# Linear attention and two MLPs on one core: chunk 1's attention moved by a step, two more tiles lent to the weight ring, x stores moved by an f tile

## The chip, the cores and the metric

One NeuronCore of a Trainium2 chip runs the program alone. The metric is the device time of an execution in microseconds (us); of several runs the median counts.

## What is computed

The reference computes, for 4 batches of 8 heads with 576 positions of 64 numbers, a linear attention and two MLPs behind it (cut):

```python
q = exp(q - q.max(-1));  q = q / (q.sum(-1) + 1e-9)       # softmax over the 64 numbers
k = exp(k - k.max(seq)); k = k / (k.sum(seq) + 1e-9)      # softmax over the positions
kv = einsum('bhsd,bhse->bhde', k, v)
x  = einsum('bhsd,bhde->bhse', q, kv)    # -> 2304 tokens x 512
h = x @ w_in                             # first MLP, 512 -> 2048
x = (s * relu(h)**2 + b) @ w_out         # 2048 -> 512
h = x @ w2_in                            # second MLP, 512 -> 2048
out = (h * tanh(softplus(h))) @ w2_out   # 2048 -> 512
```

The MLP weights come as float64 and must be used at about float32 precision.

## The kernel before

**Numbers.** The float64 weights are read as pairs of int32 and turned into float32 on the chip (`bits`, lines 132 to 144: one operation on ScalarE, four on VectorE). Each float32 operand is then split into a high part (a cast on ScalarE, line 178) and a low part (a difference on VectorE, line 175), and a product is three passes on TensorE, high by high, high by low and low by high (`passes`, line 185).

**First MLP.** The 2304 tokens are cut into five chunks (512, 256, 512, 512, 512), and the 2048 hidden numbers into 16 f tiles of 128. One f tile of one chunk is a step, 80 in all, and `n` counts them. At step n the kernel computes h of step n+2 (`emit_h`), its squared relu `r` and the split of that (`gh`, `gl`), and the y product of step n (`emit_y`), which is summed over the 16 steps of a chunk in four PSUM banks. At a chunk's end `y_out` copies the banks to `ys` and stores them to DRAM (`yd`). Sixteen weight tiles w0 to w15, of 128 x 2048 numbers (1 MB) each, hold the first MLP's weights; each holds two members, `wi` of one f tile and `wo` of another (`members`), and is read last by the last chunk at two late steps. During chunk 0 the weights arrive by SyncE's queue (`raw`), become float32 (`t`) and are split (`w`).

**Attention.** The attention of chunk c runs inside the steps of chunk c-1, for four head pairs (hp) one after the other. The stages att1 to att5 (maximum of k and q, differences and exponentials, sums, k by v on TensorE, a transpose of q to `qt`, and at last the product `x` with its copy to `xn`) are hung on steps by the table at line 855, as are the loads of k, v and q on SyncE's queue. For chunk 1 the first step of head pair hp is `2*hp+3`. `x_split` then makes `xh` and `xl` from `xn`, which the h matmuls of chunk 1 read.

**Second MLP.** Its weights are prepared on the side in the steps after 24: units of 1024 numbers a partition are read, converted, summed as a Strassen product of 2 x 2 blocks needs it, split into `umem` (in the tag w7) and stored to DRAM (`wdi` for the first, `wdo` for the second matrix) by GpSimd's queue, two stores a unit (line 332). The second MLP runs on pairs of chunks, (0, 2) and (3, 4), with seven products (P1 to P7) in place of eight: `h_unit` for each of eight tiles F, 42 matmuls of 512 columns each, and then `y_pair`. Its operands are `xoP` (x in seven combinations). Chunk 1 is done last, in the plain way.

**The ring.** The prepared weights come back in pieces `rw` of 1 MB or 768 KB, in order of use, by GpSimd's queue (lines 416 and 419). `ring_load` takes the tag that came free first, `ring_next` hands a piece out. The ring begins while chunk 4's steps run: pieces 0 and 1 go into the tags last and ws0, piece 2 into w7, which still holds `umem`; pieces 3 and 4 take last and ws0 again, and piece 5 gets ws1 when the raw y of the pair has been used there. From then on four tags go round. The tags w8 to w15 become the tiles g of F = 0 to 7, so w12 and w13 belong to F = 4 and 5.

**x of the second pair.** While the h tiles of pair 0 run, `b_steps(1, 0, put_dram)` builds the seven operands of the second pair for the lower half, splits each into `ghb` and `glb` and stores both to DRAM (line 386) on SyncE's queue. `g_tiles` gives these, and the `ghy`, `gly` of `y_pair` after them, three buffers each in turn, so that the fourth waits until the store out of the first has landed. For F from 2 to 7 this takes 1, 1, 1, 2, 2 and 1 of seven puts in the order P1, P7, P2, P6, P5, P4, P3; the upper half (`b_load(1, 1, "w7")`) is loaded behind F = 7.

The order of the instructions on each engine is made by a scheduler from these calls; instructions that go through `pin` or `keep_in_program_order` keep their order.

Of the kernel before, what the change touches and what calls it, by code (L numbers as in the profile page):

```python
# [31 lines left out]
def kernel(  # L32
# [22 lines left out]
    NF = DFF // P  # L55
# [8 lines left out]
    NU = NF // 2  # L64
# [24 lines left out]
    def segments(c):  # L89

        rq = CHUNKS[c] // P
        t, p0, found = T0[c], 0, []
        while p0 < P:
            b, s = divmod(t, S)
            n = min(P - p0, (S - s) // rq)
            found.append((b, p0, n, s))
            p0, t = p0 + n, t + n * rq
        return found


    def pin(ins):
        tc.keep_in_program_order(ins)
# [236 lines left out]
    def b_load(pair, kb, tag):  # L339

        t = (ws if tag.startswith("ws") else wp).tile([P, 4, CM], F32, tag=tag, name=f"b{pair}_{kb}")
        c0, c1 = PAIRS[pair]
        for spot, c, kk in ((0, c0, kb), (1, c0, 2 + kb), (2, c1, 2 + kb), (3, c1, kb)):
            nc.sync.dma_start(out=t[:, spot], in_=y_dram[c][:, kk, :])
        b_raw[kb] = t
# [49 lines left out]
    for pair in range(len(PAIRS)):  # L395
        ring += [("wi", F, i) for F in range(NU) for i in range(2)]
        ring += [("wo", r, i) for r in Y_ORDER for i in range(2)]
    RING = ("last", "ws0", "ws1")
    ring_t, ring_free, ring_done, ring_out = {}, ["last", "ws0", "w7"], [], set()

    def ring_load():
        ring_free.extend(ring_done)
        ring_done.clear()
        tag = ring_free.pop(0)
        if tag in ring_out:
            ring_out.discard(tag)
            return
        i = ring_at[0]
        ring_at[0] += 1
        if i >= len(ring):  # L410
            return
        t = (ws if tag.startswith("ws") else wp).tile([P, 2, 4, 2, P], F32R, tag=tag, name=f"rw{i}")
        z, a, b = ring[i]
        if z == "wi":
            o = slice(5, 8) if b else slice(0, 4)
            pin(nc.gpsimd.dma_start(out=t[:, :, 0:o.stop - o.start], in_=wi_dram[a][:, :, o]))
        else:
            t = t.rearrange("p i f h d -> p (i f h d)")
            pin(nc.gpsimd.dma_start(out=t, in_=wo_dram[b][:, BLOCK[a]].rearrange("p f i h d -> p (f i h d)")))
            t = t.rearrange("p (f i h d) -> p i f h d", f=4, i=2, h=2)  # L420
        ring_t[i] = (t, tag)

    def ring_more(tag):
        ring_free.append(tag)
        ring_load()

    def ring_next():
        t, tag = ring_t.pop(ring_at[1])
# [15 lines left out]
    def h_unit(pair, F):  # L444

        s1 = xp.tile([P, CM], F32, tag=f"xn{F % 2}", name=f"s1_{pair}_{F}")
        s2 = xp.tile([P, CM], F32, tag=f"xn{2 + F % 2}", name=f"s2_{pair}_{F}")
        s3 = rp.tile([P, CM], F32, tag="r", name=f"s3_{pair}_{F}")
        g = wp.tile([P, 4, CM], F32, tag=f"w{NU + F}", name=f"g{pair}_{F}")
        g_all[F] = g  # L450

        def mm(r, w, b):
            ps = h_bank(f"{r}_{pair}_{F}")
            for kb in range(2):
                passes(
                    ps, (w[:, kb, b, 0], w[:, kb, b, 1]), (x_op[r][:, 0, kb], x_op[r][:, 1, kb]),
                    kb == 0, kb == 1,
                )
            return ps

        def add(out, a, b):
            nc.vector.tensor_tensor(out=out, in0=a, in1=b, op=ALU.add)  # L462

        def mish(spot, src):
            nc.scalar.activation(out=g[:, spot], in_=src, func=AF.Mish)  # L465

        w = ring_next()
        p1 = mm("P1", w, 3)
        nc.scalar.copy(out=s1, in_=p1)
        p6 = mm("P6", w, 1)  # L470
        add(s2, s1, p6)
        p7 = mm("P7", w, 2)
        add(s3, s2, p7)
        p5 = mm("P5", w, 0)
        add(s2, s2, p5)
        ring_load()
        w = ring_next()
        p2 = mm("P2", w, 0)
        add(s1, s1, p2)
        mish(0, s1)  # L480
        p4 = mm("P4", w, 1)
        add(s1, s3, p5)
        mish(2, s1)
        add(s3, s3, p4)
        mish(1, s3)
        p3 = mm("P3", w, 2)
        add(s2, s2, p3)
        mish(3, s2)
        diff3(g)
        ring_load()  # L490

    TO3 = tuple(("P2", F) for F in (1, 3, 4, 5, 7)) + tuple(("P6", F) for F in (1, 3, 5))
# [62 lines left out]
    def turn(pair, k):  # L555

        j, r = divmod(k, 4)
        ps = ps_y.tile([P, DM], F32, tag=f"y{2 + k % 2}", name=f"o{pair}_{k}")
        for dr in range(2):
            for i in range(2):  # L560
                o = (2 * i + dr) * P
                nc.tensor.transpose(ps[:, o:o + P], c_all[pair][dr, j][i][:, r * P:(r + 1) * P], ident)
        if r % 2 == 0:
            o_t[pair] = cv.tile([P, 2 * DM], F32, tag=f"t{k // 2 % 2}", name=f"os{pair}_{k}")
        t = o_t[pair].rearrange("p (i d) -> p i d", i=2)
        (nc.vector.tensor_copy if r % 2 else nc.scalar.copy)(out=t[:, r % 2], in_=ps)
        if r % 2:
            rows(PAIRS[pair][j], r - 1, r + 1, t)
# [6 lines left out]
    rest_x, rest_w, rest_h, rest_g = {}, {}, {}, {}  # L575
    RN = CHUNKS[REST2]
    rest_seq = sorted([(2 * F, "wi", F) for F in range(NU)] + [(2 * F + LEAD2, "wo", F) for F in range(NU)])
    REST_TAGS = tuple(f"w{i}" for i in (0, 1, 2, 3, 4, 5, 7)) + RING

    def rest_x_load():  # L580
        t = cv.tile([P, 2 * DM], F32, tag="t0", name="rx")[:, 0:NK * RN].rearrange("p (k n) -> p k n", k=NK)
# [5 lines left out]
    def rest_load(i):  # L587
        _, z, F = rest_seq[i]
        tag = REST_TAGS[i % len(REST_TAGS)]
        t = (ws if tag.startswith("ws") else wp).tile([P, 2, 4, 2, P], F32R, tag=tag, name=f"rw_{z}{F}")  # L590
# [253 lines left out]
    def at(slot, what, fn, *args):  # L844
        todo.setdefault((slot, what), []).append((fn, args))
# [6 lines left out]
    for c in range(1, NC):  # L852
        wide = CHUNKS[c - 1] == CM
        for hp in range(NP):
            s = (c - 1) * NF + 3 * hp - 1 if c > 1 else 2 * hp + 3
            b = segments(c)[-1][0]
            if b > segments(c - 1)[-1][0]:
                first = c == 1 and hp == 0
                at(-2 if first else s - ((4 if hp else 5) if c > 1 else 2), "load", kv_load, b, hp)
                at(-2 if first else s + (0 if wide and c > 1 else 1), "load", v_load, b, hp)  # L860
            else:
                b = None
            at(-2 if c == 1 and hp < 2 else s - (2 if hp else 4), "load", q_load, c, hp)
            o = (0, 1, 2, 3, 4) if wide else (0, 1, 3, 4, 5)
            at(s + o[0], "att1", att1, b, c, hp)
            at(s + o[1], "att2", att2, b, c, hp)
            at(s + o[2], "att3", att3, b, c, hp)
            at(s + o[3], "att4_mm", att4_mm, b, c, hp)
            at(s + o[3], "att4", att4, b, c, hp)
            at(s + o[4], "att5_mm", att5_mm, b, c, hp)  # L870
# [5 lines left out]
    L0 = (NC - 1) * NF  # L876
# [11 lines left out]
    for kb in range(2):  # L888
        at(L0 + 2 * kb, "load", b_load, 0, kb, f"ws{kb}")
        for i in range(7):  # L890
            at(L0 + 2 + 5 * kb + i, "unit", b_next, kb)
    for s in (2, 9, 11):
        at(L0 + s, "load", ring_load)
    at(L0 + 14, "load", ring_more, "ws1")

    h_slot = {}
    for m in range(LEAD, NS):
# [31 lines left out]
    for n in range(NS):  # L929
        c, f = steps[n]  # L930
# [30 lines left out]

    for pair in range(len(PAIRS)):
        for F in range(NU):
            if (pair, F) == (1, 0):
                ring_more("w7")
            if F == NU - 2:
                ring_out.add("w7")
            if (pair, F) != (0, 0):
                h_unit(pair, F)
            if pair:  # L970
                turn(pair - 1, F)
            elif F == 1:
                b_load(1, 0, "w15")
                steps_b = b_steps(1, 0, put_dram)
            elif F > 1:
                for i in range((F > 4) + (F < NU - 1)):
                    next(steps_b, None)
                if F == NU - 1:
                    assert not ring_out
                    b_load(1, 1, "w7")  # L980
        if pair == 0:
            steps_b = b_steps(1, 1, put_both)
            more = [(next, steps_b)] * 7
        else:
            rest_x_load()
            more = [(rest_load, i) for i in range(7)]
        more.reverse()

        def one_more():
            fn, arg = more.pop()  # L990
            fn(arg)

        y_pair(pair, one_more)
    for i in range(7, len(REST_TAGS)):
        rest_load(i)
    for f in range(LEAD2):
        rest_h_mm(f)
    turned, loaded = 0, len(REST_TAGS)
    for f in range(NF):
# [10 lines left out]
        while loaded < len(rest_seq):  # L1010
            _, z, F = rest_seq[loaded - len(REST_TAGS)]
            if 2 * F + 1 - (LEAD2 if z == "wi" else 0) > f:
# [37 lines left out]
```

## Time and profile before

| | us |
|---|---|
| median of 3 runs | 848.21 (848.2, 848.21, 848.71) |
| the profiled execution | 845.78 |
| its span, from the first instruction to the last | 844.0 |
| TensorE (PE) busy | 821.0 (97%) |
| VectorE (DVE) busy | 605.8 (72%) |
| ScalarE (ACT) busy | 436.2 (52%) |
| GpSimd (POOL) busy | 108.7 (13%) |

All times of the trace count from the span's start in the profiled execution. PE is the matmul pipe and PEld its weight loads, SP is SyncE, and "SPq" or "POOLq" the issue of a DMA on that engine's queue. A number in square brackets behind an instruction is the time that its engine stood idle before it, and behind the arrow what ended that. Matmuls overlap a little: one of 512 columns starts 0.227 us after the one ahead of it, though each is shown as 0.39 us long. The mean granted clock of TensorE is 0.998 of full speed.

### The profile page before, as it was taken

The page shows a single profiled execution, that of the slowest core. Times are in us where ns is not written, and L with a number is a line of the kernel's source. Part 1 is how long each engine was busy: PE and PEld are TensorE (multiplying, and loading weights), DVE is VectorE, ACT ScalarE, POOL GpSimd, SP SyncE. Part 2 cuts the span into 40 slices and gives each one's busy share as a digit, 9 for nine tenths or more (in the row PEclk, how much of TensorE's full clock was granted, in tenths as well). Part 3 has the DMA queues.
Part 4 walks back from the last instruction along what each step waited for, and adds up shares of the span by engine and source line. Part 5 has one row for each costly group of instructions (what it writes and reads, how often), then busy time and mean ns, then how long its engine had stood idle before and what let it go on. Part 6 is the DMA issues. An engine that isn't in the chain of part 4 may idle for free.

```text
span 844.0 us, 11482 instructions
## 1 busy us (share of the span) xinstructions
PE 821.0 (97%) x4056; PEld 660.0 (78%) x4056; DVE 605.8 (72%) x1145; ACT 436.2 (52%) x771; POOL 108.7 (13%) x193
## 2 busy tenths in 40 slices
PE   4999999999999999999999989999999999999998
PEld 2444787998888888888888878878888888888897
DVE  7879987668677777867778656789775655976411
ACT  3636668567566566565566433455452333444322
POOL 4000000000011111111221211101111110112110
PEclk9999999999999999999999999999999999999999
DMA  8995122245465466558767498977778776688891
GB/s 219 301 365 176 33 66 92 61 151 165 158 210 196 180 216 223 185 165 273 234 210 228 144 342 236 280 257 249 233 244 262 237 199 202 218 299 283 255 373 62
DMA packets 90473, 179.01 MB, mean 212 GB/s; under 512 B 26928, under 2 KB 45104, under 8 KB 86832
## 3 DMA queue, kind: packets, MB, share of 16 engines
q0 software_dynamic: 30256, 112.73, 41.3%
q1 hardware_dynamic: 59072, 64.50, 24.5%
q10 hardware_dynamic: 1088, 1.05, 0.4%
q8 instruction: 32, 0.52, 0.2%
q14 instruction: 25, 0.20, 0.1%
HBM read 131.60 MB, written 46.66 MB: 211 GB/s over the span
## 4 chain that ended last, share of the span: by engine, by line
PE 61%; issue 27%; POOL 4%; DVE 3%; DMA 3%; ACT 1%; POOLq 0%; SPq 0%; DVEq 0%; ACTq 0%
PE P L185 24%; PE h L185 7%; PE y L185 6%; PE h L223 4%; PE y L266 3%; PE rh L185 3%; PE ry L185 3%; POOL wdo L332 2%; POOL wdi L332 2%; PE P3y L185 1%; PE P6y L185 1%; PE P5y L185 1%; PE P4y L185 1%; PE P2y L185 1%; PE P7y L185 1%
## 5 line engine op out<-in xcount | busy, mean ns | idle before, releaser
L185 PE MATMUL y<-gh,w 128*128 128x512 f32 (+1 forms) x584 | 179.6, 372 | 0.0
L185 PE MATMUL h<-xh,w 128*128 128x512 f32 (+1 forms) x568 | 173.5, 372 | 1.3 <-ACT xh L178 1.0
L185 PE MATMUL P<-xoP,rw 128*128 128x512 f32 x672 | 155.7, 390 | 2.7 <-DMA rw<-wdi 2.7
L185 PEld LDWEIGHTS P<-xoP,rw 128*128 128x128 f32 x672 | 125.8, 188 | 29.0 <-DVE s L462 3.1
L185 PEld LDWEIGHTS y<-gh,w 128*128 128x128 f32 x584 | 106.8, 189 | 18.7 <-issue 1.0
L185 PEld LDWEIGHTS h<-xh,w 128*128 128x128 f32 x568 | 104.5, 191 | 19.3 <-ACT xh L178 1.4
L462 DVE TENSOR_TENSOR s<-s,P 128x512 f32<-128x512 f32 x112 | 75.2, 686 | 51.8 <-PE P L185 35.8
L178 ACT CAST ghy_P<-g 128x512 fp32r<-128x512 f32 x112 | 69.7, 623 | 76.8 <-DVE gly_P L175 28.8
L185 PE MATMUL y<-gl,w 128*128 128x512 f32 (+1 forms) x292 | 106.9, 368 | 0.0
L185 PE MATMUL h<-xl,w 128*128 128x512 f32 (+1 forms) x284 | 105.3, 372 | 0.4 <-DVE xl L175 0.4
L175 DVE TENSOR_TENSOR gly_P<-g,ghy_P 128x512 fp32r<-128x512 f32 x112 | 76.1, 689 | 31.3 <-ACT ghy_P L178 29.2
L185 PE MATMUL P<-ghy_P,rw 128*128 128x512 f32 x224 | 87.2, 391 | 0.0
L465 ACT ACTIVATE g<-s 128x512 f32<-128x512 f32 x64 | 39.9, 632 | 89.9 <-DVE s L462 89.7
L248 ACT ACTIVATE r<-h 128x512 f32<-128x512 f32 (+1 forms) x80 | 43.9, 551 | 37.5 <-PE h L185 33.1
L185 PEld LDWEIGHTS y<-gl,w 128*128 128x128 f32 x292 | 55.1, 189 | 9.7 <-issue 0.5
L175 DVE TENSOR_TENSOR gl<-r,gh 128x512 fp32r<-128x512 f32 (+1 forms) x73 | 45.8, 629 | 21.8 <-ACT gh L178 21.5
L185 PEld LDWEIGHTS h<-xl,w 128*128 128x128 f32 x284 | 54.3, 191 | 9.2 <-DVE xl L175 0.6
L175 DVE TENSOR_TENSOR umem<-u,umem 128x512 fp32r<-128x512 f32 x64 | 41.7, 687 | 17.2 <-ACT umem L178 17.2
L178 ACT CAST umem<-u 128x512 fp32r<-128x512 f32 x64 | 36.6, 617 | 32.2 <-DVE u L319 32.0
L185 PEld LDWEIGHTS P<-ghy_P,rw 128*128 128x128 f32 x224 | 42.1, 188 | 8.4
L251 ACT ACTIVATE r<-r 128x512 f32<-128x512 f32 (+1 forms) x80 | 46.9, 589 | 1.9
L185 PE MATMUL P<-gly_P,rw 128*128 128x512 f32 x112 | 44.7, 399 | 0.3 <-DVE gly_P L175 0.3
(168 smaller groups left out, 1264.9 us busy)
## 6 DMA issues: line engine op xcount, KB each, us to landing
rw<-wdo POOLq DMA_DIRECT2D x28, 1024.0 KB, 5.2
wdi<-umem POOLq DMA_DIRECT2D x32, 512.0 KB, 3.7
wdo<-umem POOLq DMA_DIRECT2D x32, 512.0 KB, 3.7
rw<-wdi POOLq DMA_DIRECT2D x16, 1024.0 KB, 6.3
rw<-wdi POOLq DMA_DIRECT2D x16, 768.0 KB, 5.8
raw<-in_moe_w_in_dram SPq DMA_DIRECT2D x16, 512.0 KB, 9.4
raw<-in_moe_w_out_dram SPq DMA_DIRECT2D x16, 512.0 KB, 9.5
ur<-in_moe_w_in_dram SPq DMA_DIRECT2D x16, 512.0 KB, 4.2
```

The costliest lines, as they stand in the source:

```text
L175: pin(eng.tensor_tensor(out=lo, in0=src, in1=hi.bitcast(F32), op=ALU.subtract))
L178: pin(nc.scalar.copy(out=hi, in_=src))
L185: mm = nc.tensor.matmul(out=ps, lhsT=x, rhs=y, start=start, stop=stop)
L223: nc.tensor.matmul(out=h_ps[m], lhsT=wl[:, o], rhs=x_whole[kk], start=kk == 0, stop=kk == NK - 1,)
L248: op = nc.scalar.activation(out=r, in_=h_ps.pop(m), func=AF.Relu)
L251: nc.scalar.activation(out=r, in_=r, func=AF.Square)
L266: nc.tensor.matmul(out=ps, lhsT=wl[:, o], rhs=gl, start=f == 0, stop=False)
L332: nc.gpsimd.dma_start(out=to.rearrange("p b h d -> p b (h d)"), in_=u_mem[0][:, half].rearrange("p b h d -> p b (h d)"),)
L462: nc.vector.tensor_tensor(out=out, in0=a, in1=b, op=ALU.add)
L465: nc.scalar.activation(out=g[:, spot], in_=src, func=AF.Mish)
```

## The change

Three things, each by a number or a list of the plan.

- Chunk 1's attention begins at step `2*hp+2` of chunk 0 in place of `2*hp+3`, with all its loads.
- The ring begins with five pieces in five tags: last, ws0, w12 (at step 76), w13 and ws1 (at step 77). The tags w12 and w13 are used once and dropped (`ring_out`). The tag w7 joins behind F = 0 of pair 0 (before: with the third piece) and leaves at F = 6.
- The puts for F = 2 to 7 are 1, 1, 2, 2, 2 and 0, where the last call before did nothing.

```diff
--- before.py
+++ after.py
@@ -395,8 +395,7 @@
     for pair in range(len(PAIRS)):
         ring += [("wi", F, i) for F in range(NU) for i in range(2)]
         ring += [("wo", r, i) for r in Y_ORDER for i in range(2)]
-    RING = ("last", "ws0", "ws1")
-    ring_t, ring_free, ring_done, ring_out = {}, ["last", "ws0", "w7"], [], set()
+    ring_t, ring_free, ring_done, ring_out = {}, [], [], set()
 
     def ring_load():
         ring_free.extend(ring_done)
@@ -404,7 +403,10 @@
         tag = ring_free.pop(0)
         if tag in ring_out:
             ring_out.discard(tag)
-            return
+        else:
+            ring_into(tag)
+
+    def ring_into(tag):
         i = ring_at[0]
         ring_at[0] += 1
         if i >= len(ring):
@@ -419,10 +421,6 @@
             pin(nc.gpsimd.dma_start(out=t, in_=wo_dram[b][:, BLOCK[a]].rearrange("p f i h d -> p (f i h d)")))
             t = t.rearrange("p (f i h d) -> p i f h d", f=4, i=2, h=2)
         ring_t[i] = (t, tag)
-
-    def ring_more(tag):
-        ring_free.append(tag)
-        ring_load()
 
     def ring_next():
         t, tag = ring_t.pop(ring_at[1])
@@ -575,7 +573,7 @@
     rest_x, rest_w, rest_h, rest_g = {}, {}, {}, {}
     RN = CHUNKS[REST2]
     rest_seq = sorted([(2 * F, "wi", F) for F in range(NU)] + [(2 * F + LEAD2, "wo", F) for F in range(NU)])
-    REST_TAGS = tuple(f"w{i}" for i in (0, 1, 2, 3, 4, 5, 7)) + RING
+    REST_TAGS = tuple(f"w{i}" for i in (0, 1, 2, 3, 4, 5, 7)) + ("last", "ws0", "ws1")
 
     def rest_x_load():
         t = cv.tile([P, 2 * DM], F32, tag="t0", name="rx")[:, 0:NK * RN].rearrange("p (k n) -> p k n", k=NK)
@@ -852,7 +850,7 @@
     for c in range(1, NC):
         wide = CHUNKS[c - 1] == CM
         for hp in range(NP):
-            s = (c - 1) * NF + 3 * hp - 1 if c > 1 else 2 * hp + 3
+            s = (c - 1) * NF + 3 * hp - 1 if c > 1 else 2 * hp + 2
             b = segments(c)[-1][0]
             if b > segments(c - 1)[-1][0]:
                 first = c == 1 and hp == 0
@@ -889,9 +887,9 @@
         at(L0 + 2 * kb, "load", b_load, 0, kb, f"ws{kb}")
         for i in range(7):
             at(L0 + 2 + 5 * kb + i, "unit", b_next, kb)
-    for s in (2, 9, 11):
-        at(L0 + s, "load", ring_load)
-    at(L0 + 14, "load", ring_more, "ws1")
+    for s, tag in ((2, "last"), (9, "ws0"), (12, "w12"), (13, "w13"), (13, "ws1")):
+        at(L0 + s, "load", ring_into, tag)
+    ring_out.update(("w12", "w13"))
 
     h_slot = {}
     for m in range(LEAD, NS):
@@ -961,9 +959,9 @@
 
     for pair in range(len(PAIRS)):
         for F in range(NU):
-            if (pair, F) == (1, 0):
-                ring_more("w7")
-            if F == NU - 2:
+            if F == (pair == 0):
+                ring_into("w7")
+            elif F == NU - 2:
                 ring_out.add("w7")
             if (pair, F) != (0, 0):
                 h_unit(pair, F)
@@ -973,7 +971,7 @@
                 b_load(1, 0, "w15")
                 steps_b = b_steps(1, 0, put_dram)
             elif F > 1:
-                for i in range((F > 4) + (F < NU - 1)):
+                for i in range((0, 0, 1, 1, 2, 2, 2, 0)[F]):
                     next(steps_b, None)
                 if F == NU - 1:
                     assert not ring_out
```

What the scheduler makes of it stands here for three places; in these rows a number behind a name is that of the chunk, head pair or F, and a last one counts buffers.

GpSimd's queue near the end of the first MLP, before, with `umem`'s last stores (`wdo_103`) and pieces 0 to 5 of the ring:

```order
L332 DMA wdo_103<-umem 128x4x256 x2
L416 DMA rw_4026<-wdi_94 128x2x1024
L332 DMA wdo_103<-umem 128x4x256 x8
L416 DMA rw_4367<-wdi_94 128x2x768
L332 DMA wdo_103<-umem 128x4x256 x6
L416 DMA rw_4463<-wdi_95 128x2x1024
L416 DMA rw_4597<-wdi_95 128x2x768
L416 DMA rw_4629<-wdi_96 128x2x1024
```

And now:

```order
L332 DMA wdo_103<-umem 128x4x256 x2
L418 DMA rw_4026<-wdi_94 128x2x1024
L332 DMA wdo_103<-umem 128x4x256 x8
L418 DMA rw_4367<-wdi_94 128x2x768
L332 DMA wdo_103<-umem 128x4x256 x4
L418 DMA rw_4507<-wdi_95 128x2x1024
L332 DMA wdo_103<-umem 128x4x256 x2
L418 DMA rw_4549<-wdi_95 128x2x768
L418 DMA rw_4551<-wdi_96 128x2x1024
```

Piece 2 has moved ahead of the last two stores, and piece 3 (768) stands right behind them as before.

ScalarE where chunk 0 ends and chunk 1 begins, before (`ys` are the y copies of chunk 0, `xn_3` and `xh_3` the last head pair of chunk 1's x, `r` the relu of its first two h):

```order
L178 CAST w_1287<-t_458 128x2x512
L281 ACTIVATE ys_0_1235<-y_0_447,sb_s 128x512
L281 ACTIVATE ys_0_1238<-y_0_448,sb_s 128x512
L178 CAST w_1329<-t_479 128x2x512
L281 ACTIVATE ys_0_1241<-y_0_449,sb_s 128x512
L835 COPY xn_3_1118<-x_3_1115 128x256
L178 CAST xh_3_1144<-xn_3_1118 128x256
L178 CAST w_1387<-t_500 128x2x512
L281 ACTIVATE ys_0_1244<-y_0_450,sb_s 128x512
L248 ACTIVATE r_1176<-h_1163 128x256
L248 ACTIVATE r_1202<-h_1189 128x256
```

And now:

```order
L178 CAST w_1186<-t_433 128x2x512
L833 COPY xn_3_1080<-x_3_1077 128x256
L178 CAST w_1287<-t_458 128x2x512
L178 CAST xh_3_1144<-xn_3_1080 128x256
L281 ACTIVATE ys_0_1235<-y_0_447,sb_s 128x512
L281 ACTIVATE ys_0_1238<-y_0_448,sb_s 128x512
L281 ACTIVATE ys_0_1241<-y_0_449,sb_s 128x512
L178 CAST w_1329<-t_479 128x2x512
L751 ACTIVATE q_0_1042<-q_0_1042 128x512
L281 ACTIVATE ys_0_1244<-y_0_450,sb_s 128x512
L248 ACTIVATE r_1176<-h_1163 128x256
L248 ACTIVATE r_1202<-h_1189 128x256
```

The copy of `xn_3` has moved ahead of the ys and of one weight cast, an exponential of the next attention (`q_0`) ahead of the last ys, and the first `r` still stands behind all of them.

VectorE where `y_pair` of pair 0 begins, before (`glb` are the last two puts, `gly` the splits of g for P1, `s_0_7` the sums of F = 7, `g` differences of the g tiles):

```order
L175 TENSOR_TENSOR glbP_0_5123<-b_0_4727,ghbP_0_5122 128x512
L175 TENSOR_TENSOR gly_P_0_5212<-g_0_4564,ghy_P_0_5211 128x512
L462 TENSOR_TENSOR s_0_7_5129<-s_0_7_5128,P_0_7_5140 128x512
L351 TENSOR_TENSOR g_0_4564<-g_0_4564 128x512
L462 TENSOR_TENSOR s_0_7_5130<-s_0_7_5129,P_0_7_5148 128x512
L462 TENSOR_TENSOR s_0_7_5129<-s_0_7_5129,P_0_7_5156 128x512
L175 TENSOR_TENSOR gly_P_1_5222<-g_1_4660,ghy_P_1_5221 128x512
L462 TENSOR_TENSOR s_0_7_5128<-s_0_7_5128,P_0_7_5164 128x512
L175 TENSOR_TENSOR gly_P_2_5233<-g_2_4735,ghy_P_2_5232 128x512
L351 TENSOR_TENSOR g_1_4660<-g_1_4660 128x512
L351 TENSOR_TENSOR g_2_4735<-g_2_4735 128x512
L462 TENSOR_TENSOR s_0_7_5128<-s_0_7_5130,P_0_7_5156 128x512
```

And now:

```order
L175 TENSOR_TENSOR gly_P_0_5212<-g_0_4568,ghy_P_0_5211 128x512
L175 TENSOR_TENSOR gly_P_1_5222<-g_1_4664,ghy_P_1_5221 128x512
L351 TENSOR_TENSOR g_0_4568<-g_0_4568 128x512
L460 TENSOR_TENSOR s_0_7_5129<-s_0_7_5128,P_0_7_5140 128x512
L351 TENSOR_TENSOR g_1_4664<-g_1_4664 128x512
L460 TENSOR_TENSOR s_0_7_5130<-s_0_7_5129,P_0_7_5148 128x512
L175 TENSOR_TENSOR gly_P_2_5233<-g_2_4735,ghy_P_2_5232 128x512
L460 TENSOR_TENSOR s_0_7_5129<-s_0_7_5129,P_0_7_5156 128x512
L460 TENSOR_TENSOR s_0_7_5128<-s_0_7_5128,P_0_7_5166 128x512
L351 TENSOR_TENSOR g_2_4735<-g_2_4735 128x512
L460 TENSOR_TENSOR s_0_7_5129<-s_0_7_5129,P_0_7_5186 128x512
L460 TENSOR_TENSOR s_0_7_5128<-s_0_7_5130,P_0_7_5156 128x512
```

The second `gly` has moved ahead of the sums of F = 7 and the third one ahead of two of them; the sum that frees the bank of P5 (the last row of both) stands behind one more sum, and no longer behind a wait for P4's stores.

## Rows read from the trace of the kernel before

**Rows 1.** The page's part 1: busy us, share of the span, instructions.

```profile
PE 821.0 (97%) x4056; PEld 660.0 (78%) x4056; DVE 605.8 (72%) x1145; ACT 436.2 (52%) x771; POOL 108.7 (13%) x193
```

**Rows 2.** TensorE's waits: who waited for whom, us in total, times, longest.

```profile
PE P L185 <- DMA rw<-wdi: 2.7, 1, 2.7
...
PE h L185 <- ACT xh L178: 1.0, 1, 1.0
PE P1y L185 <- DVE s L462: 0.9, 1, 0.9
PE h L185 <- DVE xl L175: 0.4, 1, 0.4
```

**Rows 3.** Timeline of TensorE, 139 to 144 us.

```profile
139.15 0.71 PE L833 MATMUL x<-qt,bd 128*128 128x64 f32 x4
...
143.66 0.39 PE L185 MATMUL h<-xh,w 128*128 128x256 f32 x1 [0.31 <-ACT r L248]
```

**Rows 4.** Table by stretches: busy time of each engine, granted clock, DMA share, GB/s.

```profile
40.00:60.00 20.00, 20.00 (x48) 8.95 (x47) 16.10 (x23) 8.33 (x11) 0.00 (x0) 1.00 1.06 367
...
144.00:147.00 3.00, 3.00 (x17) 3.00 (x15) 1.72 (x4) 3.00 (x7) 0.00 (x0) 0.50 0.56 182
...
490.00:492.00 2.00, 2.00 (x9) 1.66 (x10) 0.72 (x2) 0.63 (x1) 0.00 (x0) 1.00 1.11 403
```

**Rows 5.** Timeline of TensorE, 467 to 492 us: start, us, instruction, idle before it.

```profile
467.79 0.39 PE L185 MATMUL y<-gh,w 128*128 128x512 f32 x1
...
478.45 4.24 PE L185 MATMUL P<-xoP,rw 128*128 128x512 f32 x18
...
489.94 2.31 PE L185 MATMUL P<-xoP,rw 128*128 128x512 f32 x9 [2.72 <-DMA rw<-wdi]
```

**Rows 6.** Timeline of GpSimd, 460 to 492 us.

```profile
467.09 1.50 POOL L332 DMA_DIRECT2D wdo<-umem  x2 [6.62 <-DVE umem L175]
475.23 1.50 POOL L332 DMA_DIRECT2D wdo<-umem  x2 [6.64 <-DVE umem L175]
482.40 1.42 POOL L416 DMA_DIRECT2D rw<-wdi  x2 [5.67 <-DMA wdo<-umem]
```

**Rows 7.** The page's part 6, DMA issues: count, KB each, us to landing.

```profile
rw<-wdi POOLq DMA_DIRECT2D x16, 1024.0 KB, 6.3
...
xdP<-glbP SPq DMA_DIRECT2D x7, 256.0 KB, 4.6
```

**Rows 8.** Timeline of SyncE's queue, 549 to 553 us.

```profile
550.18 1.11 SPq L386 DMA_DIRECT2D xdP<-glbP  x2
```

**Rows 9.** Timeline of VectorE, 556 to 561 us.

```profile
556.07 0.69 DVE L175 TENSOR_TENSOR gly_P<-g,ghy_P 128x512 fp32r<-128x512 f32 x1 [1.86 <-DMA xdP<-glbP]
...
559.08 1.88 DVE L462 TENSOR_TENSOR s<-s,P 128x512 f32<-128x512 f32 x3
```

**Rows 10.** Timeline of TensorE, 559 to 561 us.

```profile
559.82 0.50 PE L185 MATMUL P1y<-ghy_P,rw 128*128 128x512 f32 x1 [0.94 <-DVE s L462]
```

**Rows 11.** Timeline of ScalarE, 140 to 144 us.

```profile
140.55 0.37 ACT L835 COPY xn<-x 128x256 f32<-128x256 f32 x1
140.95 0.40 ACT L178 CAST xh<-xn 128x256 fp32r<-128x256 f32 x1
141.47 1.05 ACT L178 CAST w<-t 128x1024 fp32r<-128x1024 f32 x1
142.65 0.69 ACT L281 ACTIVATE ys<-y,sb_s 128x512 f32<-128x512 f32 x1
143.24 0.65 ACT L248 ACTIVATE r<-h 128x256 f32<-128x256 f32 x2
```

**Rows 12.** Timelines of VectorE (two rows) and TensorE (one), 49 to 132 us.

```profile
49.22 0.43 DVE L728 TENSOR_TENSOR kmx<-kb 128x256 f32<-128x256 f32 x1 [0.69 <-DMA kb<-in_k_dram]
...
127.26 2.35 DVE L175 TENSOR_TENSOR w<-t,w 128x1024 fp32r<-128x1024 f32 x2
...
131.62 0.50 PE L185 MATMUL y<-gh,w 128*128 128x512 f32 x1
```

## Prediction

> **What bounds the kernel now.** The page's first two parts come first: TensorE is busy for 97% of the span [rows 1], so there is little to win but its idle time, and no other engine's share says where that is. The table of TensorE's waits says it [rows 2]. Outside start-up three places matter: 2.7 us for a piece of the second MLP's weights (`rw`); 1.0 and 0.4 us for xh and xl where chunk 1's h matmuls begin, with 0.31 us for `r` behind them in TensorE's timeline [rows 3], 1.7 together; and 0.9 us where `y_pair` of the first pair begins. The table by stretches [rows 4] adds one cost that no wait shows: from 144 to 147 us, right behind the second of these places, the granted clock is 0.50, the lower of the two levels (1.2 GHz), so 3.0 us of work there is worth 1.5 us at 2.4 GHz. So all that can be had at the three places that the change touches is about 2.7 + 1.7 + 1.5 + 0.9 = 6.8 us.
>
> **Part by part.**
>
> *Two ring pieces into w12 and w13.* The wait of 2.72 us stands at 489.94 [rows 5]. GpSimd issues pieces 2 and 3 at 482.40 [rows 6], 5.67 us after it was ready for them, when the last store out of `umem` had landed, since piece 2 goes into that tile's tag (w7) and its queue is in order. After the change piece 2 goes into w12 and stands ahead of the last two stores, so it can be issued behind the pair at 467.09, at 468.6, if w12 is free: w13's last reader is a y matmul that ends at 468.2 [rows 5], and w12's is one step older. Landing takes 6.3 us [rows 7], so 474.9, with 12 us to spare before 487.2, where TensorE comes to it. Piece 3 follows the stores at 475.23 (476.7, in by 483). It is needed after piece 2's matmuls, so after 487.2. The whole wait of 2.7 us goes. What is late next: piece 4, in ws1, free when TensorE has done with it in the stretch from 478.45 [rows 5]; one more landing puts it at about 485, and it belongs to F=2, ten microseconds on. The tiles w12 and w13 become g of F=4 and 5, long after. Nothing is added to any engine; the count of DMAs stays. Below nothing I see no way for this term; its ends are -2.0 (some of it comes back as a shorter wait for piece 3) and -2.9, and I take **-2.7**.
>
> *x stores one f tile sooner.* Before, the four stores of the puts P4 and P3 are issued together at F=6, the low halves from 550.18 to 551.3 [rows 8], and two of the three g buffers that `y_pair` wants are theirs. VectorE stands 1.86 us for `xdP<-glbP` until 556.07, then works without a gap, and the subtraction that frees the PSUM bank of P1y is the first of three that begin at 559.08 [rows 9]; TensorE begins at 559.82 after 0.94 us [rows 10]. After, P4's stores leave at F=5 and P3's alone at F=6: `gly` of F=1 needs no store, and only that of F=2 waits, for P3's low half, issued at about 550.1 and landing after 4.6 us [rows 7], at 554.7. From there VectorE's new order has gly_2, three of the sums, one g difference and then the freeing sum: six instructions at about 0.6 us, so it ends near 558.4. TensorE is ready at 559.82 - 0.94 = 558.88. The wait goes with 0.5 us to spare. One store pair instead of two shares the queue then, which speaks for the 4.6; at the 5.9 us that the store at 550.18 took until 556.07 the sum ends at 559.7 and nothing is won. Two puts at F=5 cost VectorE and ScalarE nothing in sum. `b_load` of kb 1 goes later by about one tile of h work, since w7 is now held through F=7; its result is used by `y_pair`'s later puts, so I price it at nothing; if it were late the first `xo` put would be. Ends -0.0 and -0.9; I take **-0.9**, since the median of seven such stores stands for it and one late store against.
>
> *Chunk 1's attention one step sooner.* Nothing is added; every stage, with the DMAs of kb, v and q, moves ahead one step of chunk 0. At the border TensorE's `x` matmul of head pair 3, at 139.15 [rows 3], stands ten y matmuls sooner in the new order, each 0.227 us (18 of that size in 4.24 us with the last one's 0.39 [rows 5]), at about 136.8. Then xn and xh no longer stand behind three ys, and the waits for xh and xl (1.4 us) go. But ScalarE is in order, and the new order still has ahead of the first `r` of chunk 1, from xn at 136.9 on: xn, a weight cast, xh, three ys, another cast, an exp and the last ys. From start to next start the rows give 0.40 for xn, 0.52 for xh, 1.18 for a cast and 0.59 for a ys [rows 11]; the exp, 512 columns like a ys, I put at 0.55. That is 0.40 + 1.18 + 0.52 + 1.77 + 1.18 + 0.55 + 0.59 = 6.2 us: `r` begins near 143.1, where before it began at 143.24 and TensorE went on at 143.66 [rows 3]. So the wait does not vanish but turns into one for `r`, of 1.4 us in one piece (143.66 - 1.71 = 141.95 is where TensorE would be without any). Gain 0.2 to 0.4 us. The clock is the second half: whether it falls again to 1.2 GHz behind one wait of 1.4 us nothing in the trace decides. It fell behind 1.7 us in three pieces within 2.4 us, and it did not behind the longer wait of 2.72 us: in 490 to 492 it is 1.00 [rows 4]. I let it fall again. Ends: +1.0 (the same waits and a little more), and -3.2 (all 1.7 and the clock's 1.5). I take **-0.3**, the sum from ScalarE's rows.
>
> The Trainium skill, "TensorE: Matmul & The Clock Gate", Part 1, says that the clock follows recent activity in a window that runs freely and is not tied to the program; by it the fall behind the border could come or not from one program order to the next. The pair of places above agrees with it, a longer wait without a fall and a shorter one with it; by it the sum would be the rival below about as well as mine.
>
> Sum: -2.7 - 0.9 - 0.3 = -3.9 us. The profiled execution took 845.78 us (span 844.0 and 1.8 around it), 2.4 us less than the median 848.21; taking the difference off both, the changed kernel's profile should be near 841.9 and its median near **844.3**.
>
> **The rivals.**
>
> *The clock stays up at the border.* The lower clock's 1.5 us is then saved as well, but VectorE's new order puts the lo part of chunk 1's first g further back, behind two more attention operations and a weight difference of 1.2 us, so part of it returns as a wait for `gl`. Between 843.6 (1.0 us from this part in place of 0.3) and 842.8 (1.8, the whole of it). For it: one shorter wait. Against: any wait may do. Without any wait there (3.2) it would be 841.4.
>
> *The stores buy nothing.* The low half takes 5.9 us as one of them did, and the 0.9 stays, 845.2. For it: [rows 9]. Against: half the stores.
>
> *The ring turns into a wait for piece 3 or 4.* 845.6, with a gain of 1.4 in place of 2.7. Against it stand 4 us or more of spare time at both.
>
> *Slower: VectorE stands for k.* VectorE already waited 0.69 us for a k tile at 49.22 [rows 12], and in the new order this maximum stands ahead of the conversion of weight tile 4. The stretch 40 to 60 has the DMA engines at a share of 1.06 [rows 4], full. A step of chunk 0 is under 139.15/16 = 8.7 us. If the k tile lands no sooner, VectorE stands up to 0.69 + 8.7 = 9.4 us, and as the conversions follow one another it comes out at TensorE once it is over their slack: tile differences end at 129.61 and matmuls at 131.62 use them [rows 12], so from 2.0 us on. At the full price TensorE loses 7.4 us and, with a clock fall of 1.5, the sum is -3.6 + 8.9 = +5.3, 853.5; at half of the 7.4 it is 849.8. Against it: SyncE issues these k loads ahead of one raw pair now, so they will land sooner too.
>
> The Trainium skill, "DMA: Bandwidth & Descriptors", section "Issuing engines are not separate DMA queues", says that loads from every engine's queue run on the same 16 DMA engines and interleave; by it an earlier issue into a full stretch would not be an earlier landing in full, which speaks for the slower case. The share of 1.06 in that stretch agrees that they are full; no row shows how much a place on the queue is worth.
>
> **How the numbers follow.** My forecast, 844.3, gets 0.46; the clock that stays up 0.28 (with 841.4 inside it at 0.04); stores that buy nothing 0.12; a new ring wait 0.06; slower 0.05, of which 0.02 lands inside 0.2%; that the change leaves all as it was 0.03. A measurement of this kernel tells 0.2%, 1.7 us, from nothing: faster means below 846.5, slower above 849.9. Faster is then 0.46 + 0.28 + 0.12 + 0.06 = 0.92, less 0.03 for the cases near 846.5 and the runs' own spread of 0.5 us, 0.89; slower 0.03; the rest, 0.08, is the same. The range leaves out 841.4 and the top: 842.0 to 846.3.
>
> **What would show it.** Right: no `rw` row among TensorE's waits, piece 2 issued near 468.6; no P1y wait, and VectorE's stand before `gly` under 1 us; at the border the xh and xl waits gone and one of 1 to 1.6 us for `r`, with 3 us at 0.50 behind it. Wrong: an `h` or `y` wait for `t`, `w` or `gl` between 45 and 150 us; a wait for kb on VectorE of over 2 us; a wait for `xo` near 570.

## The result and the profile after

The changed kernel takes 841.38 us (median of 6 runs, 839.76 to 844.18), the kernel before on the same chip 849.09 us (6 runs, 848.2 to 851.24): a ratio of 0.9909 with a 95% interval from 0.9889 to 0.993. It is faster by 7.7 us, twice the 3.9 that were forecast, and 0.6 us below the range. The profiled execution took 839.76 us with a span of 838.0, so the two profiles differ by 6.0 us. One execution of all those below, of the kernel with the ring part alone, took 1184.27 us at a mean granted clock of 0.659 and is left out of every figure.

TensorE's table of waits after the change, which answers to [rows 2]:

```profile
PE h L185 <- ACT r L248: 1.4, 1, 1.4
PE y L185 <- DVE gl L175: 0.4, 1, 0.4
```

The waits for `rw`, xh, xl, P1y and gly_P are gone. What is left outside start-up is one wait for `r` and a small one for `gl`, both at the border of chunks 0 and 1. The table by stretches shows the clock, against [rows 4]:

```profile
140.00:144.00 4.00, 2.43 (x16) 1.94 (x15) 3.97 (x8) 4.00 (x8) 0.00 (x0) 1.00 0.75 247
144.00:147.00 3.00, 3.00 (x38) 2.87 (x38) 2.06 (x6) 2.33 (x6) 0.00 (x0) 1.00 0.37 125
```

From 144 to 147 us the granted clock is 1.00, where before it was 0.50. (The counts of 38 and 17 matmuls cannot be set side by side, since many of the 38 are small ones of 65 columns.) The border itself, on ScalarE (against [rows 11]):

```profile
137.58 0.37 ACT L833 COPY xn<-x 128x256 f32<-128x256 f32 x1 [1.23 <-PE x L831]
137.85 1.06 ACT L178 CAST w<-t 128x1024 fp32r<-128x1024 f32 x1
138.80 0.41 ACT L178 CAST xh<-xn 128x256 fp32r<-128x256 f32 x1
139.10 1.85 ACT L281 ACTIVATE ys<-y,sb_s 128x512 f32<-128x512 f32 x3
140.82 1.07 ACT L178 CAST w<-t 128x1024 fp32r<-128x1024 f32 x1
141.76 0.66 ACT L751 ACTIVATE q<-q 128x512 f32<-128x512 f32 x1
142.29 0.70 ACT L281 ACTIVATE ys<-y,sb_s 128x512 f32<-128x512 f32 x1
142.86 0.68 ACT L248 ACTIVATE r<-h 128x256 f32<-128x256 f32 x2
```

and on TensorE (against [rows 3]):

```profile
136.83 0.71 PE L831 MATMUL x<-qt,bd 128*128 128x64 f32 x4
...
143.32 0.39 PE L185 MATMUL h<-xh,w 128*128 128x256 f32 x1 [1.43 <-ACT r L248]
...
148.86 0.39 PE L185 MATMUL y<-gl,w 128*128 128x258 f32 x1 [0.44 <-DVE gl L175]
```

`x` is at 136.83, and ScalarE works from 137.58 without a pause up to `r` at 142.86. TensorE goes on at 143.32, 0.34 us sooner than before, and waits 0.44 us for `gl` later. GpSimd's queue at the ring's start (against [rows 6]):

```profile
467.35 1.50 POOL L332 DMA_DIRECT2D wdo<-umem  x2 [6.63 <-DVE umem L175]
468.84 0.71 POOL L418 DMA_DIRECT2D rw<-wdi  x1
475.36 1.53 POOL L332 DMA_DIRECT2D wdo<-umem  x2 [5.81 <-DVE umem L175]
476.88 0.71 POOL L418 DMA_DIRECT2D rw<-wdi  x1
478.63 1.46 POOL L418 DMA_DIRECT2D rw<-wdi  x2 [1.05 <-DVE xoP L175]
```

Piece 2 leaves at 468.84, piece 3 at 476.88, piece 4 at 478.63 with piece 5, and TensorE waits for none. The start of `y_pair`, first SyncE's queue and ScalarE, then TensorE (against [rows 8] to [rows 10]):

```profile
545.05 0.32 SPq L386 DMA_DIRECT2D xdP<-ghbP  x1
545.87 0.32 SPq L386 DMA_DIRECT2D xdP<-glbP  x1
```

```profile
549.80 0.62 ACT L178 CAST ghy_P<-g 128x512 fp32r<-128x512 f32 x1 [2.72 <-DMA xdP<-ghbP]
```

```profile
554.36 0.40 PE L185 MATMUL P1y<-ghy_P,rw 128*128 128x512 f32 x1
```

Only P3's two stores stand near the start of `y_pair` now, the high one lands 4.75 us after its issue (as ScalarE, which waits for it, shows), and TensorE comes to P1y without a wait, 5.46 us sooner than before (559.82).

### The profile page after: what moved, and what is told of

Same layout as the page of the kernel before. It is cut to its first block, busy times and chain, and to the rows that moved or that the text cites. A ratio compares the mean times of both kernels' runs of the same rounds, so it can differ in the third digit from the quotient of the medians.

```text
span 838.0 us, 11486 instructions
## 1 busy us (share of the span) xinstructions
PE 818.5 (98%) x4056; PEld 659.1 (79%) x4056; DVE 605.4 (72%) x1145; ACT 435.3 (52%) x771; POOL 108.9 (13%) x193
## 3 DMA queue, kind: packets, MB, share of 16 engines
q10 hardware_dynamic: 1088, 1.05, 0.4%
## 4 chain that ended last, share of the span: by engine, by line
PE 96%; DVE 2%; DMA 1%; issue 0%; SPq 0%; ACT 0%; DVEq 0%
PE P L185 27%; PE y L185 21%; PE h L185 20%; PE h L223 4%; PE y L266 3%; PE rh L185 3%; PE ry L185 3%; PE x L831 2%; PE kv L789 1%; PE P3y L185 1%; PE P5y L185 1%; PE P6y L185 1%; PE P1y L185 1%; PE P4y L185 1%; PE P7y L185 1%; PE P2y L185 1%
```

## The experiments

Twelve kernels ran, in three groups, each group beside runs of the kernel before on its chip: the names that begin with e (before there: median 847.68 us, 35 executions), with a or u (848.02, 23) and with x or v (848.75, 17). The kernels e1_att, e2_ring and e3_puts have one part of the change alone, u1_no_att, u2_no_ring and u3_no_puts all but one; e0_before and a0_after are the two kernels again; the last four give some stores buffers of their own. The table gives what the profiled execution of each shows: TensorE's waits at the border of chunks 0 and 1 (xh, xl, r, gl), for the ring (rw) and at the start of `y_pair` (gly_P, P1y), each summed from its table of waits. "Clock" is the time that the lower clock cost between 30 and 830 us: (1 - granted clock) x 2 us, summed over stretches of 2 us.

| kernel | border | ring | y_pair | clock | span | median, us | ratio to before (95%) |
|---|---|---|---|---|---|---|---|
| before | 1.7 | 2.7 | 1.2 | 1.7 | 844.0 | 849.09 | |
| after | 1.9 | 0 | 0 | 0 | 838.0 | 841.38 | 0.9909 (0.9889 to 0.993) |
| e0_before | 1.7 | 2.5 | 2.2 | 5.1 | 848.6 | 847.41 | 1.0003 (0.9987 to 1.002) |
| e1_att | 1.4 | 3.2 | 2.2 | 6.8 | 849.2 | 848.17 | 1.001 (0.999 to 1.0031) |
| e2_ring | 2.0 | 0 | 3.7 | 3.4 | 845.3 | 848.07 | 0.9979 (0.9951 to 1.0007) |
| e3_puts | 1.7 | 3.0 | 1.6 | 1.7 | 845.8 | 848.16 | 1.0002 (0.9985 to 1.0018) |
| a0_after | 1.9 | 0 | 1.1 | 0 | 839.0 | 840.97 | 0.9917 (0.9897 to 0.9938) |
| u1_no_att | 1.7 | 0 | 1.2 | 0 | 839.4 | 841.21 | 0.9925 (0.9904 to 0.9947) |
| u2_no_ring | 1.9 | 3.0 | 1.7 | 0 | 843.3 | 847.3 | 0.9994 (0.9978 to 1.0011) |
| u3_no_puts | 1.9 | 0.2 | 4.4 | 3.4 | 846.4 | 845.97 | 0.9965 (0.9942 to 0.9987) |
| x1_own_no_puts | 1.9 | 0 | 0 | 0 | 838.4 | 840.2 | 0.9903 (0.9876 to 0.9929) |
| x2_own_before | 1.7 | 6.8 | 0 | 5.1 | 849.0 | 845.66 | 0.9971 (0.9951 to 0.9991) |
| v4_own | 1.9 | 0 | 0 | 0 | 838.1 | 840.04 | 0.9906 (0.9879 to 0.9933) |
| v5_own_ys | 1.6 | 0 | 0 | 0 | 837.5 | 839.2 | 0.9893 (0.9864 to 0.9922) |

### The kernel before again

No edit.

> The kernel before once more, for its own spread and its granted clock. Theory A (each part is worth the wait that it takes away, and one profile of before is typical): spans near 844 with a mean clock of 0.998, ratio 1.000 within 0.2%. Theory B (behind each of the three waits the clock falls in some executions, and the profiled execution of before had fewer falls than most): spans of 844 to 849, mean clock from 0.998 down to 0.993, the longer the lower.

Its 12 executions take 844.24 to 850.61 us, at mean clocks from 1.000 to 0.994, the longer ones mostly the lower. The profiled one is of the long kind, and its table by stretches shows where the clock was lost:

```profile
490.00:493.00 3.00, 3.00 (x9) 2.31 (x8) 0.00 (x0) 0.00 (x0) 0.00 (x0) 0.50 1.11 400
...
562.00:568.00 6.00, 6.00 (x14) 4.74 (x15) 4.87 (x8) 3.59 (x6) 0.00 (x0) 0.50 0.07 29
```

Here the border of chunks 0 and 1 keeps the full clock, and the falls stand behind the other two waits: 3 us at 0.50 behind `rw`, 6 us behind the start of `y_pair`. In the execution that the prediction rests on it was the other way round. So theory B holds for the kernel before in the main (three of the twelve executions have a mean clock of 1.000, above its range): any of its three waits can be followed by a stretch at the lower level, and which it is differs from execution to execution. Over all 87 executions of the kernel before in the three groups and of this copy the mean clock is 0.9971 and the mean time 847.97 us.

### Each part alone

The earlier attention alone:

```diff
-            s = (c - 1) * NF + 3 * hp - 1 if c > 1 else 2 * hp + 3
+            s = (c - 1) * NF + 3 * hp - 1 if c > 1 else 2 * hp + 2
```

> Chunk 1's attention one step sooner alone. Theory A: 0.3 us faster as predicted (ratio 0.9996), or 2.0 us if the fall of the clock at the border goes with it (0.9976). Theory B: between the two on average (1 to 2 us, 0.998 to 0.999), one wait for r of 1.4 us in TensorE's table, the clock not below 0.99 in 140 to 160 us in most executions. The rw wait of 2.7 and the P1y wait of 0.9 us stay under both.

The x stores alone:

```diff
-                for i in range((F > 4) + (F < NU - 1)):
+                for i in range((0, 0, 1, 1, 2, 2, 2, 0)[F]):
```

> The x stores one f tile sooner alone. Theory A: the P1y wait of 0.94 and the gly wait of 0.27 us go, ratio 0.9986. Theory B: the same and up to 1.7 us of a fall of the clock behind it, 0.9966 to 0.9986. That it buys nothing (low half as late as before): 1.000 with the P1y wait still there.

The ring alone is the change with both of these lines as before.

> The two ring pieces in w12 and w13 alone. Theory A: the wait of 2.72 us goes and nothing else, ratio 0.9968. Theory B: 2.7 us and a part of a fall of the clock (up to 1.7 us) that comes behind that wait in some executions, 0.995 to 0.9965. The border's three waits stay under both.

None of the three can be told from no change: 1.001, 1.0002 and 0.9979, each interval with 1 in it. Their product is 0.999, and the whole change is 0.991. So the parts do not add up. Between theories A and B the attention and the ring alone do not decide, since their intervals hold ratios of both; neither theory had the longer wait that the ring alone shows at `y_pair`. Of the three cases for the stores alone the last came true, that they buy nothing. Attention alone has its one wait for `r` and, in the profiled execution, the lower clock behind it too (1.7 of its 6.8 us), so the fall at the border is not bound to the old order. The stores alone still wait 1.6 us for P1y: the high store issued at 550.30 let ScalarE go on at 557.53, 7.2 us later and not 4.6:

```profile
557.53 0.62 ACT L178 CAST ghy_P<-g 128x512 fp32r<-128x512 f32 x1 [5.19 <-DMA xdP<-ghbP]
```

The ring alone loses its wait of 2.7 us and has 3.7 us at `y_pair` in place of 1.2 to 2.2:

```profile
PE P L185 <- DVE gly_P L175: 2.6, 2, 2.4
...
PE P1y L185 <- DVE s L460: 1.1, 1, 1.1
```

Of its executions four lie between 842.7 and 844.2 us, seven between 847.1 and 849.4.

### All but one part

The changed kernel again:

> The changed kernel once more, for its spread and clock beside the runs of its parts. Theory B (waits plus falls of the clock that come behind them in some executions): about 841.5, mean clocks of 0.998 to 1.000, ratio 0.991 to 0.993. Theory D (the three parts add up as they were measured alone, 1.001 x 0.998 x 1.000): 0.999, and the 0.9909 belonged to those runs.

Without the earlier attention (that line as before):

> The change without the earlier attention (ring and puts together). Theory C (ring and puts are worth something only together, since the time won by the ring comes back at the start of y_pair as a wait for the stores' landing, with the clock's fall behind it): 842 to 843.5, ratio 0.993 to 0.995, no rw, P1y or gly_P wait. Theory D: 0.998, with a gly_P or P1y wait left.

Without the ring (the kernel before with the two lines above):

> The change without the two more ring pieces (attention and puts). Theory C: 847 to 848, ratio 0.999 to 1.000: the rw wait of 2.5 to 3 us stays with its falls of the clock, and P1y may still wait. Theory D: 1.001.

Without the earlier stores (the change with the second line as before):

> The change without the earlier x stores (attention and ring). Theory C: 846 to 848 in most executions, some near 842, ratio 0.996 to 0.999, with 2 to 4 us of waits for gly_P and P1y and the clock at the lower level behind them. Theory A (each wait by itself): 842.5, 0.994.

Theory D falls: the whole change gives 0.9917 on this chip too, and ring and stores together 0.9925 without the attention. Without the ring nothing measurable is left (0.9994), without the stores half is lost (0.9965). The attention's share is 0.24 us between the medians 841.21 and 840.97, as forecast in size, and too small for these intervals. Theory C holds in the main. It missed two things: in the kernel without the attention 1.2 us of the wait for P1y are left, and its time of 841.21 us is below the range; and without the stores six of twelve executions, not most, lie above 846 us (four at 842.1 or below). The profile of the kernel without the earlier stores shows how. On VectorE and TensorE at the start of its `y_pair`:

```profile
548.19 1.41 DVE L460 TENSOR_TENSOR s<-s,P 128x512 f32<-128x512 f32 x2 [0.35 <-PE P L185]
556.49 0.69 DVE L175 TENSOR_TENSOR gly_P<-g,ghy_P 128x512 fp32r<-128x512 f32 x1 [6.89 <-DMA xdP<-glbP]
```

```profile
557.24 0.58 PE L185 MATMUL P<-gly_P,rw 128*128 128x512 f32 x1 [3.79 <-DVE gly_P L175]
560.24 0.79 PE L185 MATMUL P1y<-ghy_P,rw 128*128 128x512 f32 x1 [0.58 <-DVE s L460]
```

and in its table by stretches:

```profile
558.00:564.00 6.00, 5.42 (x13) 3.49 (x12) 5.41 (x10) 3.44 (x6) 0.00 (x0) 0.50 0.02 9
```

TensorE comes to `y_pair` 4.6 us early (its first matmul there begins at 552.07, before at 556.68), by what the ring gave and by the clock, which did not fall at the border in this execution. But the low stores, issued between 545.57 and 548.15, have the g buffer that the next `gly` needs until 556.49, about the time (556.07) that they had it before. VectorE stands 6.89 us in place of 1.86, and P1y begins at 560.24, where it began at 559.82. The whole lead is lost there, and behind the longer wait 6 us run at 0.50.

The spans and mean clocks of all executions tell waits and clock apart. As an estimate, span x clock is what an execution would take at the full clock, and span x (1 - clock) what the lower clock cost (a little too much, where TensorE stood still meanwhile):

| kernel | at the full clock, us | cost of the clock, us |
|---|---|---|
| before (87 executions) | 843.8 | 2.4 |
| attention alone | 842.9 | 3.4 |
| ring alone | 841.3 | 3.4 |
| stores alone | 843.0 | 3.2 |
| ring and stores, no attention | 838.8 | 1.1 |
| attention and stores, no ring | 842.8 | 2.6 |
| attention and ring, no stores | 840.4 | 2.9 |
| whole change (a0_after) | 838.6 | 0.6 |

So the ring alone does take 2.5 us of waits away and the stores alone 0.7, but the clock costs about 1 us more in each; together they take 5.0 us, and the clock costs 1.3 us less. Of what the parts alone fall short of the two together, some 1.7 us are waits and some 3.1 us the clock, this last to about 1 us, as the executions scatter.

### The stores without the buffers

If the g buffers that wait for the stores are the cause, then other buffers for P4 and P3 should cure it with the stores as late as before. Two tiles of the convert pool are idle then:

```diff
-        hi, lo = g_tiles(f"b{r}_{kb}", CM)
+        if r in ("P4", "P3"):
+            t = cv.tile([P, 2 * DM], F32R, tag="t0" if r == "P4" else "t1", name=f"b{r}_{kb}")
+            hi, lo = t[:, 0:CM], t[:, CM:2 * CM]
+        else:
+            hi, lo = g_tiles(f"b{r}_{kb}", CM)
```

With the change less the earlier stores:

> The change without the earlier x stores, but with the operands P4 and P3 split into two buffers of the convert pool that are idle then, so that no g buffer of y_pair waits for their stores. Theory E (the ring's gain is given back because y_pair's g buffers wait for the stores to land, and the DMA engines, not TensorE, set that time): the 4.4 us of gly_P and P1y waits and the clock's two low stretches go, 841 (ratio 0.991 to 0.992), though the stores leave at F=6 as before. Rival F (the stores' traffic itself, or the order on VectorE, holds the start of y_pair up): 845 to 847, waits of over 1 us for gly_P, s or rw there.

With the kernel before:

> The kernel before with P4 and P3 in the same two idle buffers, nothing else. Theory E: the gly_P and P1y waits of 1.2 to 2.2 us go with the clock's fall behind them in some executions, while the rw wait of 2.5 to 3 us stays: 845.5 to 846.5, ratio 0.997 to 0.9985. Rival F: 848, 1.000.

With the whole change:

> The changed kernel with P4 and P3 in the two idle buffers. Theory E: the P1y wait of 1.1 us that is left in some executions goes, 840 (ratio 0.990 to 0.991), nothing else moves. Rival F: 841, 0.992.

Theory E holds. Without the earlier stores but with buffers of their own the time is 840.2 us (839.59 to 840.35), where without these buffers it was 845.97. TensorE's table shows no wait at `y_pair`. The scheduler's order on VectorE differs there too (all three `gly` stand well ahead of the last stores' splits), which follows from the buffers and was not tried apart from them. The clock stays up through the stretch that was at 0.50:

```profile
558.00:564.00 6.00, 6.00 (x28) 4.95 (x27) 6.00 (x11) 3.05 (x6) 0.53 (x1) 1.00 0.60 213
```

On the kernel before the same edit gives 0.9971, with no wait at `y_pair`. Its profile has the ring's wait at its largest:

```profile
494.02 6.25 PE L185 MATMUL P<-xoP,rw 128*128 128x512 f32 x17 [6.81 <-DMA rw<-wdi]
```

So this wait is no fixed 2.7 us: six profiles without the ring part show 2.5, 2.7, 3.0, 3.0, 3.2 and 6.8. On the whole change the edit takes the 1.1 us that were left for P1y; 840.04 is also what the kernel without the earlier stores reaches with it, so with buffers of their own no gain from earlier stores is left to see.

### Two of the four ys on VectorE

To the last kernel this is added:

```diff
-            if c == 0:
+            if c == 0 and m % 2:
+                nc.vector.tensor_scalar(out=ys, in0=ps[:, 0:w], scalar1=sb_s, scalar2=None, op0=ALU.mult)
+            elif c == 0:
```

> As the run before, and two of the four ys copies at the end of chunk 0 on VectorE, so that ScalarE has 1.2 us less ahead of the first r of chunk 1. If ScalarE's order is what sets the wait of 1.4 us for r: that wait falls to 0.2 to 0.6 us, a part comes back as a longer wait for gl (0.4 now), 839.3 to 839.8. If not: as the run before.

Its table of waits at the border:

```profile
PE h L185 <- DVE xl L175: 0.8, 1, 0.8
PE y L185 <- DVE gl L175: 0.6, 1, 0.6
...
PE h L185 <- ACT r L248: 0.2, 1, 0.2
```

The wait for `r` falls from 1.4 to 0.2 us, so it was ScalarE's order that set it. Of the 1.2 us most comes back as 0.8 for xl and 0.2 more for gl. The kernel still takes 839.2 us (839.02 to 839.46, all six below the lowest of the run before, 839.66), and the matmul that waits for gl begins at 147.69 in place of 148.54. The three waits account for 0.3 of these 0.8 us; where the rest was is not settled. This kernel has the lowest time of all the kernels here; against the changed kernel, which ran in other groups, only the ratios can be set side by side, 0.9893 and 0.9917, and their intervals overlap.

## Why the prediction was wrong

Two steps failed. The one that put the time outside the range is the clock: "I let it fall again" left the fall at the border in both kernels, and no fall was counted at the other waits. The sum of the waits came out about as forecast: in the two profiles they go from 5.6 to 1.9 us outside start-up, 3.7 less (3.9 forecast), and 1.7 us of lower clock go with them; 0.6 of the 6.0 us between the profiles stays open. The other step is to have priced the ring and the stores as independent terms. With both edits in the kernel this did not move the sum, but neither price holds by itself.

**The ring.** The mechanism was right to its times: piece 2 at 468.84 (468.6 forecast), piece 3 at 476.88 (476.7), no wait left. The term of 2.7 us was one execution's, and its independence of the stores was wrong, as the next paragraph says. The wait is 2.5 to 6.8 us in the six profiles that have it, and in four of these (the second profile of before, and those of the attention alone, the stores alone and the kernel before with the two idle buffers) 1.7 to 3.4 us are lost to the lower clock behind it.

**The x stores.** Of the three terms this one failed most in its mechanism. It was priced at 0.9 us by itself, with the ring's 2.7 us beside it, "The wait goes with 0.5 us to spare". Alone the stores give nothing measurable, since P3's high half then took 7.2 us to land, and ScalarE's cast `ghy`, ahead of the `gly` in question, waits for that half (the prediction followed the low one); even in the changed kernel 1.1 us of the wait was there in a second profile, with a landing of 6.2 us, and none in the first (4.75). But without them the ring's gain is not had either: 4.4 us of waits and 3.4 us of clock at `y_pair`. The prediction summed the terms as if each wait were at a place of its own. The place was shared: the landing of the last stores, and not TensorE, set the start of `y_pair`, so TensorE's coming sooner made that wait longer. None of the rivals had it. [rows 9] says that VectorE stood for the stores, so the question was there to be asked: does the landing move when TensorE comes sooner? The rows of before do not answer it. In the kernel without the earlier stores the issue of the low halves did move, by 4.6 us (550.18 to 545.57), and the landing did not (556.07 to 556.49). Why it did not stays open. The DMA share from 540 to 555 us was 0.98 to 1.05 before, and in the ring's new order a load of 1 MB is issued at 548.45, right behind these stores, that stood at 557.14 before. That this load holds them was not tried by itself, and it is not the whole: the stores alone, where that load is at 558.20, still took 7.2 us for one.

The Trainium skill, "DMA: Bandwidth & Descriptors", section "Issuing engines are not separate DMA queues", bears on this place more than on the one where the prediction used it: SyncE's stores and GpSimd's loads share the 16 engines. The trace agrees as far as it goes: with GpSimd's load of 548.45 right behind them, the stores issued 4.6 us sooner landed 0.4 us later.

**The earlier attention.** `x` at 136.83 (136.8 forecast), `r` at 142.86 (143.1), one wait of 1.43 us for `r` (1.4): all as worked out, and so was the wait for `gl` that the rival named. The gain is 0.24 us between medians (0.3 forecast), too small to be told from nothing, so the agreement in size may be luck. The choice "I let it fall again" was wrong for the profile: the clock stayed at 1.00. In the profile of the attention alone it fell behind the same wait. So neither is a property of the order, and the 1.7 us behind the old border were no fixed cost.

**The clock.** The prediction counted one fall, at the place where the one profile had it, and left it in both kernels. What the runs show is a mean: 0.9971 over 87 executions of the kernel before, which is 2.4 us of 846, and 0.9993 over six of the kernel after beside its parts, 0.6 us (0.9987 over the six of the result, 1.1 us). This 1.8 us (1.3 by the six of the result) is missing from the sum. With 3.0 us for the ring (the middle of its six profiles), some 1 us at `y_pair` and 0.3 at the border it gives 6.1 of the 7.0 us measured beside the parts; the remaining 0.9 is not the clock's, since at the full clock the estimate above has 5.2 us (843.8 to 838.6) where these waits make 4.3. Waits longer than these middles would make it up, of which the profile with 6.8 us shows one; which they are is not settled.

The Trainium skill, "TensorE: Matmul & The Clock Gate", Part 1, has the gate's window run freely. By it the cost of a wait should have been taken as its length and a share of a fall, at every wait. The runs agree: the same kernel had its fall at 144 us in one execution and at 490 and 562 us in another.

**The rivals.** The clock that stays up at the border came true in the profile. The stores that buy nothing came true for the stores alone. VectorE standing for k did not happen: no wait for `t` or `w` is in TensorE's table beyond the 1.5 us in start-up.

## What to carry to other kernels

When a change takes away a wait, ask of the next wait on the path whether its releaser moves too; if it is a DMA's landing that doesn't, the gain can be lost there, and two edits, neither of which could be told from no change alone, can be worth 6 us together. A part should therefore also be tested by taking it out of the whole. And one profile of a kernel whose TensorE clock differs between executions prices a wait too low or too high: profile it several times, and look at the spread of the runs, which after the change shrank from over 6 us to under 1 in the second group of runs (in the runs of the result it did not: 3.0 us over six before, 4.4 over six after).

## What the runs showed of the hardware

Waits of TensorE of 1.4 to 6.8 us were followed in some executions by 3 to 6 us at a granted clock of 0.50 (1.2 GHz) and in others by none; behind the single wait of 1.4 us for `r` this was so in one of the seven profiles that have it. With no ring wait and the stores' wait at 1.2 us or less, the mean clocks are 0.997 to 1.000 in the second and third group and six executions of a kernel lie within 0.3 to 1.7 us of each other; the first six of the changed kernel reached down to 0.996 and lie within 4.4 us.

Landing of the same 256 KB store varied between kernels and executions: 4.75 us in one execution of the changed kernel, 6.2 in another, 7.2 to 7.3 in the two kernels with the stores alone or with the attention, and 10.8 us for the first of the two low stores of the kernel without the earlier stores, whose two issues filled 2.58 us on SyncE's queue in place of 1.11.
